# Fourier mixing and a gated feed-forward layer: moved set-up products, a turned row of weights by DMA, and another order at the start of batch 1

## The chip, the cores and the metric

The kernel runs on one core of a Trainium2 chip. A core has five engines with instruction streams of their own: TensorE (PE in the profile, with its weight loads shown apart as PEld), VectorE (DVE), ScalarE (ACT), GpSimd (POOL) and SyncE (SP), which here only issues transfers. Engines meet through semaphores. Matmuls write to eight banks of accumulator memory (PSUM); DVE and ACT read the banks and write to on-chip memory. Sixteen DMA engines move data between that memory and DRAM.

The metric is the device time of one execution in microseconds. Before the change the median of three runs is 631.07 us (631.01 to 631.09).

## The reference

`x` has 8 batches of 3008 rows and 256 channels. The real part of its two-dimensional Fourier transform goes through a gated layer:

```python
X = np.fft.fft(x, axis=1)
X = np.fft.fft(X, axis=2)
y = X.real.astype(np.float32).reshape(8 * 3008, 256)
gate = np.maximum(y @ w_gate, 0.0)      # w_gate: 256 x 1536
val = y @ w_val                         # w_val:  256 x 1536
return (gate * val @ w_out).astype(np.float32)   # w_out: 1536 x 256
```

## The kernel before

**Folding.** The transform over channels is multiplied into the weights once, in the set-up: `WA[i]` holds the cosine part and `WB[i]` the sine part of the gate weights (`i` = 0) and the value weights (`i` = 1), each 128 x 1536 in bf16. The transform over rows is a set of matmuls with tables of cosines and sines (`tabC`, `tabS`) on folded input. It gives for each batch `U` (cosine part) and `V` (sine part), 128 channels by 1505 columns. A column stands for two output rows, with a plus and a minus sign of the sine part. Channel 128, which the folding leaves alone, is a row of its own: `CB` holds it for all partitions, and `b2` holds its gate weights, which are row 0 of `WB[0]`, turned so that weight `f * 128 + p` stands in partition `p`, column `f`.

**Tiles.** The 1536 hidden channels are 12 tiles of 128 (`fi` = 0 to 11; `NF` = 12). Batch 0 goes through four segments of 376 or 377 columns (`blk` = 0 to 3), batches 1 to 7 through thirds of 512, 512 and 481 columns. For each tile, PE makes a gate product and a value product (`two`, L872: a `WA` and a `WB` matmul into one bank), and a `mirror` product (L877) that turns the plus sign into the minus sign in the same bank. ACT takes the ReLU of the gate (`relu`, L888), and DVE multiplies it with the value (`mult`, L897, or `relu_mult`, L908); the second of the two multiplies reads the value bank after its mirror product and frees it (`second`, `finish`).

**Banks.** `psO` has two banks (tag `o`), `psP` two (`p`), `psV` two (`v`), `psG` and `psD` one each (`g`, `d`). In the first segment the value product uses `d` for every third tile (`fi` 2, 5, 8, 11) and `v` for the others.

**Order.** The program's order is written by hand: each engine runs its own instructions in the order in which the code emits them. `todo_out` is a list of the products with `w_out` (L781, 256 columns each, into `o`) for finished blocks; `run(todo_out, n)` emits `n` of them. Before batch 1 (`paired` is False), `run` also calls `flush`, which emits the pending evictions: `fin` (L787) copies a full bank `o` to `os` on ACT (L794) and issues the stores to the output on SP (L806). From batch 1 on, evictions come one in each tile (`run_one(evict)`).

**Extra steps of batch 0.** The dictionary `more` (L825) gives steps by (segment, tile). `weights(1)` and `weights(2)` are four steps each for the second and the last third of the weights: two matmuls of 512 columns into a bank `o` (L427), and an eviction to `WA[i]` or `WB[i]` on ACT (L433, L429) or DVE (L431). The first third is made in `dft_first`. They stand at tiles 0 to 7 of segment 0. The last third of the weights is first used at tile 8. `even_table` steps follow from tile 8 on. `gate_128` (L833) stands at (2, 2): twelve matmuls with one column, row 0 of `WB[0]` as the stationary operand and a single 1.0 as the moving one, into bank `d`, and a DVE copy to `b2`.

**The transfers of SP** run in program order. The tile layer gives them eight semaphores in turn, so that a transfer also waits for the one eight before it. Around the change SP issues the loads for batch 1, two transfers of 768 KB that reverse the rows of batch 2 (`reverse`, L180), and then the stores of batch 0's first segment.

**From batch 1 on** a tile is a `slot` (L1029). The gate product of the next tile is made apart: `sine_part` (L1012) in the bank `g`, copied to on-chip memory by ACT (L1018); `cosine_part` (L1020) onto a bank `p` that ACT has seeded with channel 128 times `b2` (`seed`, L1005, L1010); `both` (L1024) makes the sum on DVE (L1026) and the difference on POOL (L1027). `slot` gets the current tile, the next (`mid`), the one after (`nxt`), whose gate it makes, and the one after that (`after`), which it seeds. The first gates of batch 1 (`ahead[0]` and `ahead[1]`) are made in the last tile of batch 0's last segment: `single_tile` (L940) calls the steps in `extra`, then the mirror product and ReLU of its gate, then `run(todo_out, outs)`, then the steps in `last` (L1141). `lead` marks the first tile of batch 1.

Of the kernel before, what the change touches and what calls it, by code (L numbers as in the profile page):

```python
# [11 lines left out]
F32 = mybir.dt.float32  # L12
BF16 = mybir.dt.bfloat16
I32 = mybir.dt.int32
F16 = mybir.dt.float16
ALU = mybir.AluOpType
# [13 lines left out]
def dram(ap, offset, pattern):  # L30
    return bass.AP(ap.tensor, offset, [list(p) for p in pattern])
# [3 lines left out]
def kernel(  # L35
# [8 lines left out]
    nc = tc.nc  # L44
    B, S, D = x.shape
    DF = moe_w_gate.shape[1]
    NF = DF // 128
# [12 lines left out]
    psD = ctx.enter_context(tc.tile_pool(name="psD", bufs=1, space=PS))  # L60
    ctx.enter_context(tc.manual_schedule())

    def single(name, shape, dt=F32, pool=const):
        return pool.tile(shape, dt, name=name, tag=name)
# [4 lines left out]
    WB = [single(f"WB{i}", [128, DF], BF16) for i in range(2)]  # L69
# [350 lines left out]
    def weights(c):  # L420

        f = slice(c * 512, (c + 1) * 512)

        def one(i, T, W):
            p = psO.tile([128, 512], F32, name="o", tag="o")
            for kc in range(2):
                nc.tensor.matmul(p[:], lhsT=T[:, kc, :], rhs=wr[i][c][:, kc, :], start=(kc == 0), stop=(kc == 1))  # L427
            if (i, c, W) == (0, 1, WA):
                return lambda: nc.scalar.copy(W[i][:, f], p[:])  # L429
            if (i, W) in ((1, WA), (c - 1, WB)):  # L430
                nc.vector.tensor_scalar(W[i][:, f], p[:], scalar1=1.0, op0=ALU.mult, scalar2=None)  # L431
            else:
                nc.scalar.copy(W[i][:, f], p[:])  # L433
        return [lambda i=i, T=T, W=W: one(i, T, W) for i in range(2) for T, W in ((TA, WA), (TB, WB))]
# [22 lines left out]
    for t in range(3):  # L457
        n = ROWS[1][t]
        p = slice(0, n)
# [43 lines left out]
    start_pool.__exit__(None, None, None)  # L503
    ch128 = nc.dram_tensor("ch128", (B, 4 * NJ + 1), BF16, kind="Internal").ap()
    b2 = single("b2", [128, NF])
    one = single("one", [1, 1], BF16)
    nc.vector.memset(one[:], 1.0)


    def even_table(n, c):  # L510
# [50 lines left out]
    def flush():  # L561
        for todo in (evict, sums):
            while todo:
                todo.pop(0)()
# [257 lines left out]
    fold_even()  # L822
    turns_and_rows()

    more = {(0, i): [s] for i, s in enumerate(weights(1) + weights(2))}  # L825
    for n, c in enumerate(even_order):
        for k, step in enumerate(even_table(n, c)):
            more.setdefault(divmod(EVEN_AT[n] + k, NF), []).append(step)
# [1 line left out]
    for seg in (2, 3):  # L830
        more.setdefault((1, 8 + seg), []).append(lambda seg=seg: minus_v(nc.scalar, seg))

    def gate_128():  # L833
        p = psD.tile([128, 512], F32, name="d", tag="d")
        for f in range(NF):
            nc.tensor.matmul(p[:, f:f + 1], lhsT=WB[0][0:1, f * 128:(f + 1) * 128], rhs=one[:], start=True, stop=True)
        nc.vector.tensor_scalar(b2[:], p[:, 0:NF], scalar1=1.0, op0=ALU.mult, scalar2=None)
    more[(2, 2)] = [gate_128]
    more_1 = {}
    for at, step in zip((-5, -4, -3, -2, -1, 7, 7, 8, 14, 17), channel_loads() + channel_turn()):  # L840
        (more_1 if at >= 0 else more).setdefault(at if at >= 0 else (3, NF + at), []).append(step)
# [5 lines left out]
    todo_out, todo_dft, todo_fold = [], [], []  # L847
# [3 lines left out]
    def run(todo, n):  # L851
        for _ in range(min(n, len(todo))):
            todo.pop(0)()
        if not paired:
            flush()

    def run_one(todo):
        if todo:
            todo.pop(0)()

    def run_fold(us):

        nonlocal credit
        credit = credit + us if todo_fold else 0
        while todo_fold and credit >= todo_fold[0][0]:
            cost, step = todo_fold.pop(0)
            step()
            credit -= cost
        if us > 50:
            credit = 0  # L870
# [6 lines left out]
    def mirror(bank, st, i):  # L877

        W, v = (WB, st["vm"]) if st["b"] == 0 else (WM, st["vs"])
        nc.tensor.matmul(bank[:, 0:st["n"]], lhsT=W[i][:, st["f"]], rhs=v, start=False, stop=True, skip_group_check=True)  # L880

    def bank(tag):
        return {"g": psG, "p": psP, "v": psV, "d": psD}[tag].tile([128, 512], F32, name=tag, tag=tag)
# [4 lines left out]
    def relu(st):  # L888
        st["r"] = space()
        nc.scalar.activation(st["r"][:, 0:st["n"]], st["g"][:, 0:st["n"]], ACTF.Relu)  # L890

    def half_h(st, sign):

        n = st["n"]
        return st["h"][:, 2 * n - 1:n - 1:-1] if sign else st["h"][:, 0:n]

    def mult(st, sign, r=None):  # L897
        n = st["n"]
        nc.vector.tensor_tensor(half_h(st, sign), (r or st["r"])[:, 0:n], st["v"][:, 0:n], op=ALU.mult)  # L899
# [8 lines left out]
    def relu_mult(st, sign):  # L908
        n = st["n"]
        nc.vector.scalar_tensor_tensor(half_h(st, sign), in0=st["s"][1 + sign][:, 0:n], scalar=0.0, in1=st["v"][:, 0:n],  # L910
                                       op0=ALU.max, op1=ALU.mult)

    def second(st):
        (relu_mult if "s" in st else mult)(st, 1)
        if st["n"] == 481:
            keep_rest(st)

    def finish(st):
        mirror(st["v"], st, 1)
        second(st)  # L920

    def value(st):
        st["v"] = bank("v")
        two(st["v"], st, 1)

    def gate(st, tag="g"):
        st["g"] = bank(tag)
        two(st["g"], st, 0)
        relu(st)
# [10 lines left out]
    def single_tile(st, outs, extra=(), last=(), tag="p"):  # L940

        gate(st, tag)
        if pending is not None:
            finish(pending)
        value(st)
        mult(st, 0)
        run(todo_out, outs)
        for step in extra:
            step()
        mirror(st["g"], st, 0)  # L950
        relu(st)
        run(todo_out, outs)
        for step in last:
            step()
        return st

    def first_tile(st, extra, outs):
# [47 lines left out]
    def seed(st, p=None):  # L1005

        if st is None or st["kind"] == "o":
            return
        st["p"] = p or bank("p")
        nc.scalar.activation(st["p"][:, 0:st["n"]], st["c"], ACTF.Copy, scale=b2[:, st["fi"]:st["fi"] + 1])  # L1010

    def sine_part(st):  # L1012
        n = st["n"]
        st["g"] = bank("g")
        nc.tensor.matmul(st["g"][:, 0:n], lhsT=WM[0][:, st["f"]], rhs=st["vs"], start=True, stop=True)  # L1015
        q = space()
        st["s"] = q, space(), q
        nc.scalar.copy(q[:, 0:n], st["g"][:, 0:n])  # L1018

    def cosine_part(st):  # L1020
        n = st["n"]
        nc.tensor.matmul(st["p"][:, 0:n], lhsT=WA[0][:, st["f"]], rhs=st["us"], start=False, stop=True, skip_group_check=True)  # L1022

    def both(st):  # L1024
        n, (q, sp, sm) = st["n"], st["s"]
        nc.vector.scalar_tensor_tensor(sp[:, 0:n], in0=q[:, 0:n], scalar=-0.5, in1=st["p"][:, 0:n], op0=ALU.mult, op1=ALU.add)  # L1026
        nc.gpsimd.tensor_tensor(sm[:, 0:n], sp[:, 0:n], q[:, 0:n], op=ALU.add)  # L1027

    def slot(cur, mid, nxt, after, outs, fold_us):  # L1029

        stop = len(todo_out)

        def out(part):
            run(todo_out, len(todo_out) - stop + outs * part // 8)
        old = nxt is not None and nxt["kind"] == "o"
        new = nxt is not None and not old
        if old:
            gate(nxt)
        lead = cur["lead"]
        if lead:  # L1040
            out(5)
        if new and mid["kind"] != "o":
            sine_part(nxt)
        out(3 if not lead else 5)
        out(5)
        if new and mid["kind"] == "o":
            sine_part(nxt)
        if new:
            cosine_part(nxt)
        seed(after)  # L1050
        if pending is not None:
            mirror(pending["v"], pending, 1)
        if pending is not None:
            second(pending)
        value(cur)
        if cur["kind"] == "o":
            mult(cur, 0, cur["first"])
        else:
            relu_mult(cur, 0)
        if new:  # L1060
            both(nxt)
        if old:
            nxt["first"] = nxt["r"]
            mirror(nxt["g"], nxt, 0)
            relu(nxt)
        run_fold(fold_us)
        run_one(evict)
        run_one(sums)
        out(8)
        return cur  # L1070
# [4 lines left out]
    for b in range(B):  # L1075
# [4 lines left out]
        for blk, block in enumerate(blocks):  # L1080
# [44 lines left out]
            if (b, blk) == (0, 0):  # L1125
                for fi in range(NF):
                    st = tile_of(block, fi, (U, V, CB))
                    add_h(st, hs)
                    if fi == 8:
                        todo_out = out_steps(b, block, hs, True)  # L1130
# [3 lines left out]
            elif not paired:  # L1134
                for fi in range(NF):
                    st = tile_of(block, fi, (U, V, CB))
                    add_h(st, hs)
                    tag = {(3, 8): "g", (3, 9): "d", (3, 10): "g", (3, 11): "d"}.get((blk, fi), "p")
# [8 lines left out]
                    if (blk, fi) == (1, 8):  # L1147
                        run(todo_out, len(todo_out))
                        todo_out = out_steps(b, block, hs, True)
                    pending = single_tile(st, 3 if blk == 1 else per_tile // 2, more_b.get((blk, fi), ()), last, tag)  # L1150
                    run(todo_dft, DFT_0[blk - 1][fi])
            else:
                for fi in range(NF):
# [4 lines left out]
                    outs = per_tile  # L1158
                    if (b, blk) == (B - 1, 2) and fi > 8:
                        outs = (10, 11, 17)[fi - 9]  # L1160
# [12 lines left out]
            if (b, blk) == (B - 1, 2):  # L1173
                todo_out = rest
            elif b or blk > 1:
                todo_out = out_steps(b, block, hs)
# [36 lines left out]
```

## Time and profile before

| | us |
|---|---|
| median of 3 runs | 631.07 |
| the profiled execution | 630.98 |
| its span in the profile | 629.2 |
| PE busy in it | 620.5 (99%) |
| DVE busy | 551.5 (88%) |
| POOL busy | 502.7 (80%) |
| ACT busy | 445.5 (71%) |

The span runs from the first to the last instruction of the program that the profiler shows; 1.8 us of the execution lie around it. In rows of the timeline the columns are start and length in microseconds, engine, line, operation, what it writes and reads, shapes, and how many instructions were merged into the row; in brackets the idle time of the engine ahead of it and what ended it. Matmuls are pipelined: the length of a row reaches to the modelled end of the matmul, while the next one has begun long before. So two starts have to be compared to see what a matmul costs. Batch 0 lies between about 19 and 104 us, batch 1 begins at about 105 us.

### The profile page before, as it was taken

The numbers are of one execution on the slowest core, as the hardware profiler recorded it, in microseconds if no ns is written. First come the engines' busy times: TensorE is split into PE (matmuls) and PEld (weight loads), VectorE is DVE, ScalarE is ACT, GpSimd is POOL, SyncE is SP. The second block draws the span as 40 slices with busy tenths as digits, with TensorE's granted clock in tenths as the row PEclk, the third lists the DMA queues.
The fourth block names the chain that finished last, engine by engine and source line by source line (L and its number), as shares of the span: only waits on it lengthen the run. The fifth ranks groups of instructions, "written<-read, shape, count | busy, mean of one in ns | idle before, by whom it ended". The sixth has DMA issues, their size and how long they took to land.

```text
span 629.2 us, 12441 instructions
## 1 busy us (share of the span) xinstructions
PE 620.5 (99%) x4114; PEld 398.4 (63%) x4114; DVE 551.5 (88%) x981; ACT 445.5 (71%) x813; POOL 502.7 (80%) x478
## 2 busy tenths in 40 slices
PE   8999999999999999999999999999999999999997
PEld 2566666566666666666666666666666666666666
DVE  8886676999899899988999999899999989999991
ACT  7796667777777767777777777777777777777762
POOL 8887992898999988799979989699886566666660
PEclk9999999999999999999999999999999999999999
DMA  9953748734264327315362426211221111211113
GB/s 240 209 206 118 173 177 102 182 73 151 82 150 145 126 76 183 113 44 165 83 187 64 140 76 130 68 50 36 77 61 38 42 60 56 57 38 51 51 44 102
DMA packets 82911, 66.47 MB, mean 106 GB/s; under 512 B 38517, under 2 KB 65941, under 8 KB 82846
## 3 DMA queue, kind: packets, MB, share of 16 engines
q1 hardware_dynamic: 78260, 60.01, 34.3%
q0 software_dynamic: 3984, 4.92, 3.9%
q10 hardware_dynamic: 602, 0.75, 0.4%
q8 instruction: 32, 0.52, 0.4%
q14 instruction: 33, 0.27, 0.2%
HBM read 41.88 MB, written 34.16 MB: 121 GB/s over the span
## 4 chain that ended last, share of the span: by engine, by line
PE 91%; DVE 4%; issue 2%; POOL 1%; DMA 1%; ACT 1%; DVEq 0%; ACTq 0%; POOLq 0%
PE o L781 36%; PE v L880 10%; PE v L875 9%; PE v L874 9%; PE g L1015 8%; PE p L1022 8%; PE d L585 4%; DVE h L910 2%; PE p L880 1%; PE p L874 1%; PE p L875 1%; DMA XG<-in_x_dram,gidx 1%; DVE h L899 1%; DVE r L1026 1%; POOL XG L120 1%
## 5 line engine op out<-in xcount | busy, mean ns | idle before, releaser
L1027 POOL TENSOR_TENSOR r<-r 128x512 f32<-128x512 f32 (+1 forms) x251 | 313.2, 1254 | 100.5 <-DVE r L1026 98.1
L910 DVE SCALAR_TENSOR_TENSOR h<-r,v 128x512 bf16<-128x512 f32 (+1 forms) x502 | 317.1, 673 | 39.2 <-PE v L880 26.5
L781 PE MATMUL o<-wo,h 128*128 128x256 bf16 x2172 | 330.6, 272 | 0.0
L781 PEld LDWEIGHTS <-h 128*128 128x128 bf16 x2220 | 216.7, 98 | 112.0 <-issue 1.3
L1010 ACT ACTIVATE p<-CB,b 128x512 f32<-128x512 bf16 (+1 forms) x251 | 171.8, 684 | 73.4 <-DVE r L1026 72.1
L1018 ACT COPY r<-g 128x512 f32<-128x512 f32 (+1 forms) x251 | 145.1, 578 | 66.5 <-PE g L1015 57.4
L1026 DVE SCALAR_TENSOR_TENSOR r<-r,p 128x512 f32<-128x512 f32 (+1 forms) x251 | 167.9, 669 | 0.9 <-ACT r L1018 0.9
L875 PE MATMUL v<-V,WB 128*128 128x512 bf16 (+3 forms) x296 | 108.6, 367 | 0.0
L874 PE MATMUL v<-U,WA 128*128 128x512 bf16 (+3 forms) x296 | 108.6, 367 | 0.0
L880 PE MATMUL v<-V,WM 128*128 128x512 bf16 (+1 forms) x252 | 94.4, 375 | 0.8 <-DVE h L910 0.4
L1015 PE MATMUL g<-V,WM 128*128 128x512 bf16 (+1 forms) x251 | 94.1, 375 | 0.5 <-ACT r L1018 0.4
L1022 PE MATMUL p<-U,WA 128*128 128x512 bf16 (+1 forms) x251 | 94.1, 375 | 0.2 <-ACT p L1010 0.2
L899 DVE TENSOR_TENSOR h<-r,v 128x376 bf16<-128x376 f32 (+2 forms) x90 | 46.2, 546 | 17.6 <-PE v L880 10.1
L874 PEld LDWEIGHTS <-WA 128*128 128x128 bf16 x348 | 33.9, 97 | 39.5 <-issue 10.4
L875 PEld LDWEIGHTS <-WB 128*128 128x128 bf16 x348 | 34.0, 98 | 34.3 <-DVE WB L431 0.6
L794 ACT COPY os<-o 128x512 f32<-128x512 f32 x92 | 52.6, 571 | 3.5 <-issue 3.0
L198 POOL TENSOR_TENSOR XG<-XG,XD 128x510 f32<-128x510 f32 x42 | 53.0, 1270 | 0.8 <-DMA XG<-xr 0.8
L890 ACT ACTIVATE r<-p 128x376 f32<-128x376 f32 (+1 forms) x80 | 38.0, 486 | 17.8 <-PE p L880 9.0
L206 POOL TENSOR_TENSOR AA<-XG 128x510 f32<-128x510 f32 x42 | 45.5, 1093 | 0.0
L1015 PEld LDWEIGHTS <-WM 128*128 128x128 bf16 x251 | 24.6, 98 | 5.7 <-issue 0.3
L1022 PEld LDWEIGHTS <-WA 128*128 128x128 bf16 x251 | 24.5, 98 | 3.7 <-issue 0.8
L880 PEld LDWEIGHTS <-WM 128*128 128x128 bf16 x253 | 24.8, 98 | 3.1
(186 smaller groups left out, 412.3 us busy)
## 6 DMA issues: line engine op xcount, KB each, us to landing
out_dram<-os SPq DMA_DIRECT2D x124, 128.0 KB
xr<-in_x_dram SPq DMA_DIRECT2D x12, 768.0 KB
XG<-xr SPq DMA_DIRECT2D x12, 768.0 KB
XD<-in_x_dram SPq DMA_DIRECT2D x15, 512.0 KB
out_dram<-os SPq DMA_DIRECT2D x35, 112.0 KB
XD<-in_x_dram SPq DMA_DIRECT2D x8, 448.0 KB
CB<-ch SPq DMA_DIRECT2D x7, 376.2 KB
out_dram<-os SPq DMA_DIRECT2D x13, 96.0 KB
```

Source lines behind the costliest of these rows:

```text
L198: e.tensor_tensor(XG[p, r, t, ::-1, 1:D], XG[p, r, t, ::-1, 1:D], XD[p, r, t, :, D - 1:0:-1], op=ALU.add)
L781: nc.tensor.matmul(st["p"][0:m, q, :], lhsT=lhs(f), rhs=wo[:, f, :], start=(f == 0 and not (early and q)), stop=(f == NF - 1), skip_group_ ...
L874: nc.tensor.matmul(bank[:, 0:st["n"]], lhsT=WA[i][:, st["f"]], rhs=st["us"], start=True, stop=False)
L875: nc.tensor.matmul(bank[:, 0:st["n"]], lhsT=WB[i][:, st["f"]], rhs=st["vs"], start=False, stop=True)
L880: nc.tensor.matmul(bank[:, 0:st["n"]], lhsT=W[i][:, st["f"]], rhs=v, start=False, stop=True, skip_group_check=True)
L910: nc.vector.scalar_tensor_tensor(half_h(st, sign), in0=st["s"][1 + sign][:, 0:n], scalar=0.0, in1=st["v"][:, 0:n], op0=ALU.max, op1=ALU.mult)
L1010: nc.scalar.activation(st["p"][:, 0:st["n"]], st["c"], ACTF.Copy, scale=b2[:, st["fi"]:st["fi"] + 1])
L1015: nc.tensor.matmul(st["g"][:, 0:n], lhsT=WM[0][:, st["f"]], rhs=st["vs"], start=True, stop=True)
L1018: nc.scalar.copy(q[:, 0:n], st["g"][:, 0:n])
L1022: nc.tensor.matmul(st["p"][:, 0:n], lhsT=WA[0][:, st["f"]], rhs=st["us"], start=False, stop=True, skip_group_check=True)
L1026: nc.vector.scalar_tensor_tensor(sp[:, 0:n], in0=q[:, 0:n], scalar=-0.5, in1=st["p"][:, 0:n], op0=ALU.mult, op1=ALU.add)
L1027: nc.gpsimd.tensor_tensor(sm[:, 0:n], sp[:, 0:n], q[:, 0:n], op=ALU.add)
```

## The change

Three things are changed.

1. `weights(2)` goes from tiles 4 to 7 of segment 0 to tiles 3 to 6. Tile 3 has two steps then, the last of `weights(1)` and the first of `weights(2)`.
2. `gate_128` goes, with its operand `one` and the memset that fills it. Instead, row 0 of `WB[0]` is stored to DRAM (`wrow`, 1536 values of 2 bytes) by a transfer that SP issues at tile (1, 1); at (1, 4) a second transfer reads it back so that each partition gets its 12 values (`brow`, 128 x 12), and at (2, 2) ACT copies `brow` to `b2`.
3. In the last tile of batch 0 the evictions are emitted after the steps of `last` instead of before them. In the slot of batch 1's first tile, `cosine_part` and `seed` come after the mirror and value products of the tile and its first multiply, instead of before them. For all other tiles `slot` and `single_tile` emit what they did, in the same order.

```diff
-    one = single("one", [1, 1], BF16)
-    nc.vector.memset(one[:], 1.0)
+    wrow = nc.dram_tensor("wrow", (1, DF), BF16, kind="Internal").ap()
+    brow = single("brow", [128, NF], BF16)
...
-    more = {(0, i): [s] for i, s in enumerate(weights(1) + weights(2))}
+    more = {(0, i): [s] for i, s in enumerate(weights(1))}
+    for i, step in enumerate(weights(2)):
+        more.setdefault((0, 3 + i), []).append(step)
...
-    def gate_128():
-        p = psD.tile([128, 512], F32, name="d", tag="d")
-        for f in range(NF):
-            nc.tensor.matmul(p[:, f:f + 1], lhsT=WB[0][0:1, f * 128:(f + 1) * 128], rhs=one[:], start=True, stop=True)
-        nc.vector.tensor_scalar(b2[:], p[:, 0:NF], scalar1=1.0, op0=ALU.mult, scalar2=None)
-    more[(2, 2)] = [gate_128]
+    more[(1, 1)].append(lambda: nc.sync.dma_start(out=wrow, in_=WB[0][0:1, :]))
+    more[(1, 4)].append(lambda: nc.sync.dma_start(out=brow[:], in_=dram(wrow, 0, [[1, 128], [128, NF]]), allow_slow_non_contiguous=True))
+    more[(2, 2)] = [lambda: nc.scalar.copy(b2[:], brow[:])]
...
         mirror(st["g"], st, 0)
         relu(st)
-        run(todo_out, outs)
+        for _ in range(outs):
+            run_one(todo_out)
         for step in last:
             step()
+        run(todo_out, 0)
         return st
...
         lead = cur["lead"]
-        if lead:
-            out(5)
+        out(4 if lead else 0)
         if new and mid["kind"] != "o":
             sine_part(nxt)
-        out(3 if not lead else 5)
-        out(5)
+        out(4 if lead else 5)
         if new and mid["kind"] == "o":
             sine_part(nxt)
-        if new:
+        if new and not lead:
             cosine_part(nxt)
-        seed(after)
+        if not lead:
+            seed(after)
         if pending is not None:
             mirror(pending["v"], pending, 1)
         if pending is not None:
@@
             mult(cur, 0, cur["first"])
         else:
             relu_mult(cur, 0)
+        if lead:
+            out(5)
+            cosine_part(nxt)
+            seed(after)
         if new:
             both(nxt)
```

With six products of `todo_out` for each tile there, `out(4)` and `out(5)` both mean three of them, so that the first three stay ahead of the sine product and the rest at the end of the slot.

## The prediction

> **What bounds the kernel now.** I read the shares of the page first, then its chain of waits, then the list of who waited for whom on TensorE up to 150 us, then the timeline of each place in that list.
>
> ```profile
> span 629.2 us, 12441 instructions
> PE 91%; DVE 4%; issue 2%; POOL 1%; DMA 1%; ACT 1%; DVEq 0%; ACTq 0%; POOLq 0%
> ```
>
> TensorE (PE) carries 91% of the chain that ends last. A microsecond taken out of PE's stream is therefore a microsecond of the kernel, unless something with a clock of its own holds PE later. The waits of PE (total, times, longest) between 0 and 150 us that this change can touch are these:
>
> ```profile
> PE g L1015 <- ACT r L1018: 0.4, 1, 0.4
> PE p L1022 <- ACT p L1010: 0.2, 1, 0.2
> PE d L875 <- DVE WB L431: 0.2, 1, 0.2
> ```
>
> They look small because a matmul's row lasts until its modelled end. The start of the next one shows the loss. With no wait, matmuls of 376 columns start 0.16 us apart, of 512 columns 0.21 to 0.22, of 256 columns (the `o` products) 0.11. The timeline of PE, tile 8 of batch 0's first segment, then DVE there:
>
> ```profile
> 29.94 0.32 PE L880 MATMUL p<-CB,WB 128*128 128x376 bf16 x1
> 30.10 0.32 PE L874 MATMUL d<-U,WA 128*128 128x376 bf16 x1
> 30.63 0.33 PE L875 MATMUL d<-V,WB 128*128 128x376 bf16 x1 [0.20 <-DVE WB L431]
> 28.98 0.53 DVE L899 TENSOR_TENSOR h<-r,d 128x376 bf16<-128x376 f32 x1
> 29.89 0.68 DVE L431 TENSOR_SCALAR WB<-o 128x512 bf16<-128x512 f32 x1
> ```
>
> The product due at 30.10 + 0.16 = 30.26 starts at 30.63, just behind the last eviction of weights (29.89 + 0.68 = 30.57). Loss: 0.37 us. The second place is the turning of channel 128's weights:
>
> ```profile
> 63.98 0.38 PE L781 MATMUL o<-wo,h 128*128 128x256 bf16 x2
> 64.29 0.45 PE L836 MATMUL d<-one,WB 1*128 1x1 bf16 x12
> 64.67 0.33 PE L880 MATMUL p<-CB,WB 128*128 128x376 bf16 x1
> ```
>
> The two `o` products are through at 63.98 + 0.21 = 64.19, and the next full product starts at 64.67: 0.48 us. The third is the start of batch 1, PE and then ACT:
>
> ```profile
> 104.74 0.49 PE L781 MATMUL o<-wo,h 128*128 128x256 bf16 x3
> 105.66 0.38 PE L1015 MATMUL g<-V,WM 128*128 128x512 bf16 x1 [0.44 <-ACT r L1018]
> 106.25 0.38 PE L1022 MATMUL p<-U,WA 128*128 128x512 bf16 x1 [0.21 <-ACT p L1010]
> 106.47 0.32 PE L880 MATMUL v<-CB,WB 128*128 128x377 bf16 x1
> 107.87 0.38 PE L1015 MATMUL g<-V,WM 128*128 128x512 bf16 x1
> 104.53 0.59 ACT L794 COPY os<-o 128x512 f32<-128x512 f32 x1
> 105.00 0.62 ACT L1018 COPY r<-g 128x512 f32<-128x512 f32 x1
> 105.47 0.73 ACT L1010 ACTIVATE p<-CB,b 128x512 f32<-128x512 bf16 x1
> ```
>
> The `o` products end at 104.74 + 0.33 = 105.07. The sine product waits 0.60 us for the copy that frees the one bank `g`, the cosine product another 0.37 for the seed of its bank. The eviction L794 stands ahead of both on ACT.
>
> **The change part by part. Weights a tile sooner.** Nothing is added: products of the last third move from tiles 4 to 7 into tiles 3 to 6, so tile 3 now has two groups. All positions from here are followed by hand with the spacing of rows: ACT copy 0.49 us before its successor starts, ReLU 0.38 to 0.40, DVE eviction 0.60, DVE multiply 0.46. Tile 3's second pair runs from 23.86 to 24.28; its input had landed by about 21. ACT gets a second copy at 24.55, and tile 4's ReLU moves from 24.55 to about 25.04. PE asks for that ReLU only at 26.15 (tile 4's mirror product), so the delay is hidden, with 0.6 us to spare. The DVE evictions of WA and WB fall to about 27.35 and 28.87, and the last weights are ready near 29.55 instead of 30.57.
>
> What is late next is bank `d`, which tile 8's value product reuses. It is freed by the DVE multiply that reads `d` (28.98 above). That multiply now has both evictions ahead of it and ends near 30.0. PE, with tile 7's pair gone and tile 3's added, reaches that product at about 30.03 and may wait 0.1; its second half then starts at 30.26. Gain **0.37**; with `d` half a microsecond later than I have it, nothing. The next input, `wo`, issued at 15.1, takes 15.1 us to land, at 30.2; its first use moves from 30.80 to 30.43, still behind it.
>
> **Twelve one-column products out.** PE gets 0.48 us back, but the mirror product that follows waits for a ReLU like those of the neighbouring tiles (a loss of 0.04 to 0.09 there), so I take **0.43**, with 0.38 (64.29 to 64.67 alone) and 0.48 as ends. A 0.16 us DVE copy goes. A 128x12 ACT copy comes, which no row shows; the 128x2 ones of L451 take 0.19, so 0.2. It stands on ACT between two ReLUs. The one ahead is needed by the mirror product and is not delayed; the one behind waits for that product anyway (0.4 to 0.9 us idle before these ReLUs). Cost: 0. The one-element memset of 0.06 us on DVE at 17.0 goes as well; I count nothing for it.
>
> **Two transfers in.** SP is idle from 32.3 on, so the 3 KB store of the row is issued there, a few microseconds after its last writer, and lies behind the two 768 KB transfers issued at 30.77. The read back is 1536 separate elements of 2 bytes. SP reaches it only after the sixth store of batch 0's outputs; it also waits for the row and for the transfer eight before it, so about 45.9:
>
> ```profile
> 45.15 0.70 SPq L806 DMA_DIRECT2D out_dram<-os  x2
> 52.13 0.82 SPq L806 DMA_DIRECT2D out_dram<-os  x2
> 101.50 6.08 SPq L133 DMA_DIRECT2D CX<-in_x_dram  x4
> ```
>
> [...] SP's next job is at 52.13. Four output buffers and about 5 us of slack cover it: cost 0. What it feeds is read at 64.2 at the earliest. [...]
>
> **Batch 1's first tile.** No instruction is added. The eviction L794 goes behind the next copy and seed on ACT. In the same hand count, the copy for tile 1 is at 104.74 (as soon as its product, begun at 104.31, is out) and ends at 105.34, so tile 2's sine product starts at 105.38 instead of 105.66. Behind it stand now the products that need nothing from ACT: mirror 105.59, value 105.75 and 105.97. Tile 2's seed runs 105.21 to 105.94 meanwhile, and the cosine product follows at 106.18 without a wait. Then three `o` products to 106.71, three of the transform to 107.19, and the next sine product at 107.19 instead of 107.87: **0.68**. Next in line: its bank is free at 106.93 (copy of tile 2 behind the eviction), its seed ends near 107.5 against a need at 107.7, and the eviction, 1.3 us later, feeds a store that SP could issue only at 107.6. If ACT came 0.4 us later, 0.28 would remain.
>
> Sum: 0.37 + 0.43 + 0.68 = **1.48 us**. Between the three places I found only waits that follow PE itself; the loads with their own clock have slack (the row `CB` for batch 1, issued at 91.80, is first read at 100.06). The profiled execution took 630.98 (span 629.2 and 1.8 around it), 0.09 under the median of 631.07. So 631.07 - 1.48 = **629.6 us**.
>
> **Rivals.** (A) *The weights' wait only changes its name*: bank `d` in place of WB. For it: DVE is busy without a gap from 27.9 to 32, and both evictions go ahead of the freeing multiply. Against: my count has 0.1 us. It leaves 1.48 - 0.37 = 1.11: about 630.0.
> (B) *The start of batch 1 keeps half its wait*: ACT has five jobs from 104.74 to 107.5 and PE one `g` bank. Price: only 0.28 of 0.68 is gained, so 1.08 in all, and 630.0.
> [...]
> (D) *More than the sum*: waits at 37.82, 43.04 and 60.54 (0.1 to 0.4 us each, for ACT and DVE) shrink with the new phase: 629.2.
>
> **How the numbers follow.** What a measurement of this kernel tells from no change is put at 0.2%, 1.26 us: faster means under 629.81. My forecast has 0.55, with 629.3 to 629.9 as its own range; about five sixths of it lies under the bound. A has 0.14, B 0.16 (both mostly within the bound), C 0.05, D 0.10. Faster 0.57, same 0.37, slower 0.06. The range reaches over A, B and D, and over A and B together (1.48 - 0.37 - 0.40, 630.4): 629.1 to 630.6.
>
> **What would show it.** Right: tile 8's second value product 0.16 to 0.25 us behind its first, no row of twelve 1x1 products and about 1.45 us between mirror products there, the first sine and cosine products of batch 1 without a wait of over 0.1 us, and every later stage earlier by 1.5. Wrong: a PE wait on the reader of `d` near 30; an ACT wait on DMA near 64; a new PE wait in the first four tiles of batch 1; or an advance of 0.8 us at 70 us that is gone by 100, which would mean that a load or POOL, not PE, sets the pace there.

## The result and the profile after

Over 14 runs each, the kernel before takes 631.00 us (630.84 to 631.25) and the changed one 629.87 (629.54 to 630.15): 1.13 us less, a ratio of 0.9981 with a 95% interval from 0.9974 to 0.9988. The forecast was 629.6, a gain of 1.48. The changed kernel's profiled execution took 629.88, with a span of 628.1 against 629.2. Its page, the first line and the chain that ended last:

```profile
span 628.1 us, 12374 instructions
PE 93%; DVE 3%; issue 1%; ACT 1%; DMA 1%; DVEq 0%; ACTq 0%
```

PE carries the chain still more than before (91%). The list of who waited for whom on PE, cut to 0 to 150 us (total, times, longest), without its lines for the start and for loads:

```profile
PE v L879 <- DVE h L898: 0.5, 2, 0.3
PE p L879 <- ACT r L889: 0.2, 1, 0.2
PE v L879 <- DVE h L909: 0.2, 1, 0.2
```

The three waits that the change was aimed at (on `g`, on the seed of `p`, on `WB`) are gone from this list. By the starts of the matmuls 0.29 us are still lost on `g`, as the prediction had it (105.07 to 105.38 there); e8_fill below takes that up. The wait on DVE's multiply (0.2 us, once, before the change) now makes 0.5 us in two. First the three places, in the timeline of the changed kernel, PE's rows and then those of DVE and ACT:

```profile
30.09 0.32 PE L873 MATMUL d<-U,WA 128*128 128x376 bf16 x1
30.24 0.32 PE L874 MATMUL d<-V,WB 128*128 128x376 bf16 x1
...
62.33 0.32 PE L879 MATMUL p<-CB,WB 128*128 128x376 bf16 x1
63.81 0.32 PE L879 MATMUL p<-CB,WB 128*128 128x376 bf16 x1
...
104.26 0.49 PE L781 MATMUL o<-wo,h 128*128 128x256 bf16 x3
104.88 0.38 PE L1016 MATMUL g<-V,WM 128*128 128x512 bf16 x1
105.68 0.38 PE L1023 MATMUL p<-U,WA 128*128 128x512 bf16 x1
106.71 0.38 PE L1016 MATMUL g<-V,WM 128*128 128x512 bf16 x1
...
28.90 0.68 DVE L431 TENSOR_SCALAR WB<-o 128x512 bf16<-128x512 f32 x1
29.50 0.53 DVE L898 TENSOR_TENSOR h<-r,d 128x376 bf16<-128x376 f32 x1
...
63.66 0.19 ACT L837 CAST b<-brow 128x12 f32<-128x12 bf16 x1
...
104.24 0.58 ACT L1019 COPY r<-g 128x512 f32<-128x512 f32 x1
104.72 0.70 ACT L1011 ACTIVATE p<-CB,b 128x512 f32<-128x512 bf16 x1
105.35 0.59 ACT L794 COPY os<-o 128x512 f32<-128x512 f32 x1
```

Tile 8's two products start 0.15 us apart instead of 0.53. The mirror products on both sides of the twelve one-column products are 1.48 us apart, as tiles without them are (1.95 before). At the start of batch 1 the sine product comes 0.62 us behind the first `o` product instead of 0.92, and the next sine product 1.83 us after it instead of 2.21.

What each place gave is read best as an *advance*: the start of a matmul in the profile before, less the start of the same matmul in the profile after.

| at (time in before) | advance, us | what lies between |
|---|---|---|
| 29.5 | 0.04 | |
| 30.8 | 0.40 | the weights: 0.36 |
| 65.06 | 0.87 | the one-column products: 0.47 |
| 67.2 | 0.42 | lost: 0.45 |
| 108.4 | 1.16 | the start of batch 1, with 0.06 regained before it |
| 200 | 0.95 | lost near 172: 0.2 |
| 250 to 550 | 1.18 to 1.15 | won near 222: 0.23 |
| 600 | 1.37 | won near 566: 0.22 |
| 617 | 1.00 | lost near 616: 0.37 |

Five of these rows (67.2, and all from 200 on) are about things the prediction did not speak of. The loss at 67 is the largest, and the timeline of the changed kernel shows where it begins, on DVE (PE, DVE, ACT):

```profile
64.91 0.32 PE L874 MATMUL v<-V,WB 128*128 128x376 bf16 x1
65.82 0.32 PE L874 MATMUL p<-V,WB 128*128 128x376 bf16 x1
66.44 0.32 PE L879 MATMUL v<-CB,WB 128*128 128x376 bf16 x1 [0.29 <-DVE h L898]
63.54 1.00 DVE L898 TENSOR_TENSOR h<-r,v 128x376 bf16<-128x376 f32 x2 [0.48 <-PE v L879]
65.38 1.00 DVE L898 TENSOR_TENSOR h<-r,v 128x376 bf16<-128x376 f32 x2 [0.84 <-PE v L874]
64.17 1.02 ACT L889 ACTIVATE r<-p 128x376 f32<-128x376 f32 x2 [0.32 <-PE p L879]
```

The multiply of 65.38 needs the first of the two ReLUs of 64.17, out at 64.66, and a value product of PE whose mirror partner is out by 64.91. Its wait, which the trace records as a semaphore instruction of its own, is met at 64.97. The multiply one tile earlier started 0.05 us behind its wait; this one starts 0.41 behind, 0.36 more. The bracket of its row names PE's product of 64.91, whose modelled end is 65.23; in e5_pad below the same multiply starts before that product's end, so it does not wait for it. From 64.97 on DVE waits for nothing that the profile shows. PE, which wants the result, starts its mirror product 0.62 us behind the last product (65.82 to 66.44) where 0.16 is the pitch.

### The profile page after: what moved, and what is told of

Same layout as the page of the kernel before. It is cut to its first block, busy times and chain, and to the rows that moved or that the text cites. A ratio compares the mean times of both kernels' runs of the same rounds, so it can differ in the third digit from the quotient of the medians.

```text
span 628.1 us, 12374 instructions
## 1 busy us (share of the span) xinstructions
PE 617.9 (98%) x4057; PEld 398.2 (63%) x4102; DVE 550.9 (88%) x979; ACT 445.8 (71%) x814; POOL 502.7 (80%) x478
## 4 chain that ended last, share of the span: by engine, by line
PE 93%; DVE 3%; issue 1%; ACT 1%; DMA 1%; DVEq 0%; ACTq 0%
PE o L781 37%; PE v L874 10%; PE v L879 10%; PE g L1016 8%; PE p L1023 8%; PE v L873 8%; PE d L585 4%; DVE h L909 2%; PE p L879 1%; PE p L873 1%; PE p L874 1%; PE v L395 1%; DMA XG<-in_x_dram 1%; DVE h L898 1%; DVE r L1027 1%
## 5 line engine op out<-in xcount | busy, mean ns | idle before, releaser
L873 PE MATMUL v<-U,WA 128*128 128x512 bf16 (+3 forms) x254 | 92.7, 365 | 0.0
L889 ACT ACTIVATE r<-p 128x376 f32<-128x376 f32 (+1 forms) x80 | 38.0, 486 | 17.8 <-PE p L879 9.6
```

What stands on the lines that cost most here:

```text
L873: nc.tensor.matmul(bank[:, 0:st["n"]], lhsT=WA[i][:, st["f"]], rhs=st["us"], start=True, stop=False)
```

## The experiments

In all of them a run of the kernel before stood on the same chip. "Late start" means: an instruction of DVE that begins about 0.40 us behind its wait although nothing that it reads is missing.

### e1_again: the changed kernel once more

No edit.

> The changed kernel once more, unedited, for a second profile. In the first one the advance over before is 0.39 us behind the weights, 0.85 behind the twelve products that went, but only 0.42 to 0.54 from 66.4 us on: DVE began one multiply at 65.38 although its waits had been met at 64.97, and PE waited 0.46 us for it at 66.44. Theory 'chance': such a late start (0.4 us) falls anywhere in an execution, and in another one it is elsewhere; then the advance between 67 and 100 us is 0.80 to 0.87 here. Rival 'place': it belongs to this spot of the changed program; then the advance is again 0.4 to 0.55 there. Time of both: 629.6 to 630.1, ratio 0.9975 to 0.9987.

629.93 us against 631.01, ratio 0.9982 [0.9973, 0.9991]. The advance goes -0.16, 0.19, 0.66 (65.06), 0.22 (67.2), 0.96 (108.4), 0.99 (250) to 0.85 (617). The first value is the start-up, which differs by 0.20 us between these two executions of one kernel (and by up to 0.6 us between the profiles of this document) and has nothing to do with the change; the steps after it are those of the first profile to within 0.04 us. The loss at 67 and the late multiply (65.58 here) belong to the kernel, not to one execution.

### e2_weights, e3_transfers, e4_start: each part alone, on the kernel before

```diff
e2:  -    more = {(0, i): [s] for i, s in enumerate(weights(1) + weights(2))}
     +    more = {(0, i): [s] for i, s in enumerate(weights(1))}
     +    for i, step in enumerate(weights(2)):
     +        more.setdefault((0, 3 + i), []).append(step)
e3:  the change's lines on one, wrow, brow, gate_128 and more[(1, 1)], more[(1, 4)], more[(2, 2)]
e4:  the change's lines in single_tile and slot
```

> Only the weights a tile sooner. Theory of the sum: 0.37 us faster, ratio 0.9994, with the value product of tile 8 at 30.24 and no loss behind it. Rival A (bank d takes the wait over): 0 to 0.15 us, and a PE wait for DVE near 30.

> Only the turning of channel 128's weights by transfers. Theory of the sum: 0.43 us faster, ratio 0.9993, and the advance of 0.4 to 0.46 holds from 65 us to the end. Rival 'place': the multiply behind it starts late again, 0.05 to 0.15 us faster, ratio 0.9998 or more. [...]

> Only the other order at the end of batch 0 and the start of batch 1. Theory of the sum: 0.68 us faster, ratio 0.9989 (in the first profile of the whole change the advance there grew by 0.62). Rival B: 0.28, ratio 0.9996.

| | median, us | before | ratio [95%] | advance |
|---|---|---|---|---|
| e2_weights | 630.64 | 631.01 | 0.9994 [0.9986, 1.0003] | 0.02, then 0.38 from tile 8 to the end (0.41) |
| e3_transfers | 630.82 | 631.01 | 0.9997 [0.9988, 1.0006] | -0.15, 0.32 at 65.06, -0.12 at 67.2, 0.06 at the end |
| e4_start | 630.20 | 631.01 | 0.9990 [0.9981, 0.9998] | 0.18, 0.86 at 108.4, 1.13 at the end |

Two of the three intervals reach 1, so the times alone do not show these parts; the steps of the advance do. The weights and the start of batch 1 are worth what they are worth in the whole change, 0.36 and 0.68 (the other 0.27 of e4_start's advance at the end come at 222, 320 and 566 us, taken together, and belong to what follows). The transfers win 0.47 and lose 0.44 again within 2.2 us, by themselves. So the loss at 67 is no collision of the three parts; it comes with the second. The timeline of e3_transfers, DVE and PE:

```profile
65.92 1.00 DVE L896 TENSOR_TENSOR h<-r,v 128x376 bf16<-128x376 f32 x2 [0.84 <-PE v L872]
66.98 0.32 PE L877 MATMUL v<-CB,WB 128*128 128x376 bf16 x1 [0.29 <-DVE h L896]
```

It is the same late multiply. To see what it has in common with others I numbered DVE's instructions, waits included, in the order of the traces. In the changed kernel late starts stand at numbers 191, 447, 703, 1343 and 1599 (65.38, 170.12, 269.97, 515.16, 614.17 us); before at 319, 575 and 1471 (119.30, 220.75, 564.98); in e2 at the same three numbers; in e3 at 191 and 959; in e4 at 831. DVE's rows in the kernel before:

```profile
119.30 0.69 DVE L910 SCALAR_TENSOR_TENSOR h<-r,v 128x512 bf16<-128x512 f32 x1 [0.30 <-PE v L875]
220.75 0.69 DVE L910 SCALAR_TENSOR_TENSOR h<-r,v 128x512 bf16<-128x512 f32 x1 [0.93 <-PE v L875]
564.98 0.69 DVE L910 SCALAR_TENSOR_TENSOR h<-r,v 128x512 bf16<-128x512 f32 x1 [0.42 <-PE v L875]
```

Every one is 63 plus a multiple of 128, right behind a wait. The changed kernel's trace has 13 such places. At the eight others nothing is seen: three are waits themselves (575, 959, 1471), and at five DVE goes on without idle time (63, 319, 831, 1087, 1215). Not every late start costs PE time: those at 119.30 before and at 269.97 and 515.16 after leave the advance as it is.

ACT has them too, which speaks against a cause in DVE's data. Its copy of `g` starts 0.04 us behind its wait as a rule. In the changed kernel one starts 0.32 behind (its wait met at 148.44, its start at 148.76), and that is ACT's instruction 319, again 63 plus a multiple of 128; in the kernel before it is 319 as well (149.60 to 149.92), in e3_transfers 575 and 831, in e4_start 1087 and 1215. The bracket of its row names POOL, but the distance is 0.32 at every one of these places. The timeline of the changed kernel, ACT:

```profile
148.76 0.58 ACT L1019 COPY r<-g 128x512 f32<-128x512 f32 x1 [1.07 <-POOL r L1028]
```

A second view points the same way, the list of DMA queues on the changed kernel's page (packets, MB, share of 16 engines):

```profile
q8 instruction: 32, 0.52, 0.4%
q14 instruction: 33, 0.27, 0.1%
```

33 loads of 0.27 MB are 8 KB each. They are not DVE's alone: the trace holds 4190 instructions of DVE, ACT, POOL and SP together, and 33 times 128 is 4224. The trace's DMA records give their times: one begins at 66.06, 170.90, 270.81 and 614.82, each 0.65 to 0.85 us *after* one of the late starts, and one at 516.51, 1.35 us after the fifth. This tie is loose: behind the late start at 119.30 of the kernel before, the next load begins only 3.2 us later. The theory from here on is an estimate from these counts, 63 plus multiples of 128 and 33 loads of 8 KB; no trace shows it as such: DVE's code comes in blocks of 128 instructions, the first instruction of a block starts 0.40 us behind its wait instead of 0.05, and this shows only where that instruction has just been waited for. The change took one memset and one copy out of DVE's stream and added one wait, so every instruction behind 64 us moved by one in the count.

### e5_pad: the changed kernel with the dropped memset kept

```diff
+    one = single("one", [1, 1], BF16)
+    nc.vector.memset(one[:], 1.0)
```

Nothing reads `one`. The rival was that ACT's new copy, or the order around it, holds the multiply.

> The changed kernel with one more DVE instruction in the set-up (the one-element memset at 17 us stays; nothing reads it). Theory 'code block': the late multiply is the DVE instruction that begins a block of 128 in DVE's stream (191st in the profiles of the changed kernel, of its repeat and of the transfers alone, each time right after a wait); one instruction more puts the wait itself there. Then no DVE row starts 0.4 us after its met wait at 65 us, the advance over before is 0.80 to 0.87 from 65 to 100 us and 1.4 to 1.5 behind the start of batch 1, and the late starts at 170, 270, 515 and 614 us go, while those of before at 220 and 565 us come back. Time 1.45 us under before, ratio 0.9977. Rival 'the ACT copy': the copy to b2 on ACT delays the multiply, wherever the instruction stands; then nothing changes: ratio 0.9982, late start at 65.4.

629.50 us against 631.06, ratio 0.9975 [0.9965, 0.9984]. The timeline of e5_pad, DVE and PE:

```profile
63.57 1.00 DVE L900 TENSOR_TENSOR h<-r,v 128x376 bf16<-128x376 f32 x2 [0.48 <-PE v L881]
65.05 1.00 DVE L900 TENSOR_TENSOR h<-r,v 128x376 bf16<-128x376 f32 x2 [0.48 <-PE v L881]
66.10 0.32 PE L881 MATMUL v<-CB,WB 128*128 128x376 bf16 x1
```

Number 191 is now the wait itself, and the multiply behind it starts 0.05 us after it. The late starts at 170, 270, 515 and 614 us are gone, and the three of the kernel before (319, 575, 1471) are back, as expected. PE's mirror product comes 0.25 us behind its predecessor, without a wait in brackets. The advance is 0.01, 0.36, 0.83, 0.75 (67.2), 1.44 (108.4) and 1.44 at the end. One instruction *more* on DVE, with the copy on ACT left in place, makes the kernel faster: the rival falls.

### e6_transfers_pad: the second part alone, with the memset kept

The edit is e3's without the removal of `one`.

> Only the transfers, with that memset kept. Code block: 0.40 to 0.45 us faster than before instead of 0.19, ratio 0.9993, advance 0.4 held from 65 to 100 us; a late start is possible at the 447th, 703rd, 831st, 1343rd or 1599th DVE instruction (about 170, 270, 320, 515 and 615 us). Rival ACT copy: 0.19 again.

630.68 us against 631.06, ratio 0.9995 [0.9986, 1.0003]. The advance is 0.30, 0.76, 0.68 (67.2) and 0.68 until 150: the loss of 0.36 is away. Then 0.48 (200), 0.72 (250 to 550), 0.94 and 0.57: with late starts at 447, 703, 1343 and 1599 it has the later losses of the changed kernel. Two late starts of e3_transfers (191 and 959) are gone and four others have come, so the time alone would not have shown the step.

### e7_slot_only: the third part without the eviction's move

The new order in `slot`, but `single_tile` as before, so that ACT's eviction stays ahead of the copy of `g`.

> Of the start of batch 1 only the slot's order, with the evictions of the last tile flushed where they were before. The eviction stays ahead of the copy that frees bank g, so the sine product waits as before (0.60 us), but the cosine product does not wait for its seed any more (0.37). Theory: 0.35 to 0.4 us faster, ratio 0.9994; the flush then accounts for the other 0.3. Rival: the eviction is not what holds ACT, and the whole 0.6 to 0.8 comes from the slot: ratio 0.9988.

630.48 us against 631.06, ratio 0.9990 [0.9982, 0.9999]. In its timeline PE still waits for the copy:

```profile
105.44 0.38 PE L1015 MATMUL g<-V,WM 128*128 128x512 bf16 x1 [0.43 <-ACT r L1018]
```

The advance grows by 0.37 there (0.23 to 0.60) instead of 0.68. So 0.37 of the third part is the place of the cosine product and of the seed, and the 0.31 left are the eviction, which was not moved alone.

### e8_fill: e5 with all six `o` products ahead of the first sine product

After the change, 0.29 us are still lost at 104.88 (three `o` products from 104.26 are through at 104.59). Three products more fill them:

```diff
-        out(4 if lead else 0)
+        out(8 if lead else 0)
```

> The changed kernel with the memset kept, and in the first slot of batch 1 all six output products ahead of the sine product instead of three. In the changed kernel that product still waits 0.30 us for the copy that frees bank g; the three products that fill the wait come from the end of the slot. Theory: 0.2 to 0.3 us under the changed kernel with the memset alone, ratio 0.9973 of before. Rival: the next sine product, then 0.32 us sooner, waits for its own bank instead: same time as with the memset alone.

629.11 us against 631.06, ratio 0.9971 [0.9960, 0.9982], the lowest median of all, though its interval and e5's overlap. The timeline of e8_fill, PE:

```profile
103.62 0.82 PE L783 MATMUL o<-wo,h 128*128 128x256 bf16 x6
104.27 0.38 PE L1018 MATMUL g<-V,WM 128*128 128x512 bf16 x1
105.08 0.38 PE L1025 MATMUL p<-U,WA 128*128 128x512 bf16 x1
105.83 0.38 PE L1018 MATMUL g<-V,WM 128*128 128x512 bf16 x1
```

The sine product follows six `o` products without a gap (103.62 to 104.27, 0.108 us each). The start gives 0.87 instead of 0.68, and the advance stays at 1.99 to 2.01 to the end. Of this 0.46 is the start-up of that execution (at 29.5), and the weights gave only 0.27 there: PE's first product with `wo` comes at 30.08, just behind the load of `wo`, which was issued at 15.3 and took 14.7 us to land. The 0.19 over e5 at the start of batch 1 is what this edit shows.

### e9_pad_late: the memset at 70 us instead of 17

```diff
+    one = single("one", [1, 1], BF16)
...
+    more.setdefault((2, 8), []).append(lambda: nc.vector.memset(one[:], 1.0))
```

> The changed kernel plus one memset of one element on DVE (a tile that nothing reads), as in e5, but placed near 70 us, after DVE's instruction 191, instead of at 17 us. Theory (what counts is how many instructions stand before a place in DVE's stream): the multiply near 65.4 us is still 0.40 us late (instruction 191 is not moved) and PE still loses 0.36 us more than before at 66.4; everything behind the memset moves by one, so the late starts near 170, 270, 515 and 614 us go and those near 220 and 564 of the kernel before return. Advance over the kernel before about 1.1 us from 108 us to the end; median 629.8 to 629.9, so 0.3 to 0.4 above e5. Rival (the memset at 17 us itself, or the layout of the start, is what helped e5): the late starts stay where the changed kernel has them, near 170, 270, 515 and 614 us; or the one near 65.4 goes too.

629.87 us against 630.89, ratio 0.9982 [0.9973, 0.9991]. The timeline of e9_pad_late shows late starts in four places (DVE, then PE):

```profile
65.50 1.00 DVE L900 TENSOR_TENSOR h<-r,v 128x376 bf16<-128x376 f32 x2 [0.84 <-PE v L876]
118.25 0.69 DVE L911 SCALAR_TENSOR_TENSOR h<-r,v 128x512 bf16<-128x512 f32 x1 [0.30 <-PE v L876]
219.70 0.69 DVE L911 SCALAR_TENSOR_TENSOR h<-r,v 128x512 bf16<-128x512 f32 x1 [0.92 <-PE v L876]
563.93 0.69 DVE L911 SCALAR_TENSOR_TENSOR h<-r,v 128x512 bf16<-128x512 f32 x1 [0.42 <-PE v L876]
66.56 0.32 PE L881 MATMUL v<-CB,WB 128*128 128x376 bf16 x1 [0.29 <-DVE h L900]
```

Ahead of the memset the changed kernel's late start is kept, with its loss (0.75 to 0.30); behind it the four of the changed kernel are gone and the three of the kernel before are back. The advance is 1.05 from 107 us to the end. It is the count of instructions ahead of a place that decides, not what the memset does at the start.

### e10_before_pads: the kernel before with its memset issued four times

```diff
-    nc.vector.memset(one[:], 1.0)
+    nc.vector.memset(one[:], 1.0)
+    nc.vector.memset(one[:], 1.0)
+    nc.vector.memset(one[:], 1.0)
+    nc.vector.memset(one[:], 1.0)
```

> The kernel before, unchanged but for the one-element memset at 17 us, which is issued four times instead of once (three more instructions of 0.06 us each on DVE). Theory: DVE's instruction 191 is now the multiply that started at 63.93 us in the kernel before, right behind its wait; it starts 0.40 us late, DVE's copy of the bias, the ReLUs behind it and the next pair of multiplies follow 0.40 us later, and PE's mirror product at 66.86 comes 0.3 to 0.4 us late. A late start of 0.40 us also appears at instruction 959, near 365 us, as in e3, and one near 614 us (1599). The late starts near 220 and 564 us stay. The kernel is 0.7 to 1.1 us slower than before: 631.7 to 632.1. Rival (three memsets cost their own time at most, at a place where DVE waits): no late start at 64 us, advance between -0.2 and 0.0 from 20 us to the end, median 631.0 to 631.2.

630.55 us against 630.89, ratio 0.9992 [0.9983, 1.0001]. I had expected a slower kernel, 631.7 to 632.1; it is not slower, and if anything faster. The timeline of e10_before_pads, DVE and PE:

```profile
64.46 1.00 DVE L903 TENSOR_TENSOR h<-r,v 128x376 bf16<-128x376 f32 x2 [0.84 <-ACT r L894]
369.56 0.69 DVE L914 SCALAR_TENSOR_TENSOR h<-r,v 128x512 bf16<-128x512 f32 x1 [0.42 <-POOL AA L206]
65.38 0.32 PE L879 MATMUL p<-V,WB 128*128 128x376 bf16 x1
65.54 0.32 PE L884 MATMUL v<-CB,WB 128*128 128x376 bf16 x1
```

The late starts at 191, 959 and 1599 (613.02) came where they were expected, 0.40 to 0.41 us behind their waits (64.05 for the first). PE lost nothing at any of them. At 64.46 a reason can be read, though no run tested it: the two multiplies are out at 65.46, and PE's mirror product that needs them comes at 65.54, and the twelve one-column products, still in this kernel, have held PE by 0.48 us. My price was wrong in a second point: I thought the late starts near 220 and 564 would stay, but three more instructions move those too. With them gone the advance goes from -0.16 to 0.07 at 222 and 0.28 at 566. Three memsets that do nothing for the result move the advance by 0.44, as much as one part of the change, through where the late starts fall; the time itself (0.34 us less) has an interval that reaches 1.

## Why the prediction was right, and where it was not

**Faster by a little: right, by less than the likeliest case had it.** 629.87 lies in the range (629.1 to 630.6) and 0.27 above the forecast. The gain is 1.13 us of 1.48. The prediction called faster what is under 629.81 and gave that 0.57; 629.87 is just on the other side, among the cases with 0.37. What the prediction left out cost 0.44 of the advance here and nothing in e5; which of the two comes hangs on one instruction, so it was chance that the loss stayed small enough for the range.

**Weights a tile sooner: 0.37 foreseen, 0.36 in the changed kernel, 0.36 in e2.** The DVE eviction is at 28.90 (28.87 worked out) and the reader of `d` ends at 30.03 (near 30.0). Rival A falls: PE goes from 29.90 to 30.09, so at most 0.03 us is lost on `d`.

**Twelve products out: 0.43 foreseen, 0.47 at 65.06.** It is 0.39 when the tiles behind it have settled (the 0.08 between 65.06 and 67.2 of e5), inside the ends of 0.38 and 0.48 that were given. ACT's copy cost 0, for the reason given: it sits between two ReLUs at 63.66.

**The transfers: cost 0, right.** SP issued the read at 46.01 (45.9 worked out) in 0.39 us, and the trace's DMA records show its 1536 pieces moved between 47.2 and 50.1 us. For the slack of about 5 us behind that cost, no run ahead of the result shows how long such an issue takes; the changed kernel showed 0.39 us, and 5.33 us from its end to SP's next store (46.40 to 51.73; that store was at 52.13 before). The copy that needs the read is at 63.66, with 13 us to spare: the late read to which the forecast gives 0.05 as C is shown by no run. What the prediction did not have is how late the row itself came: its store was issued from 32.35 on, its 3072 bytes moved only at 45.42, and the read waited for them (the list of who waited for whom on SP's queue, 25 to 60 us):

```profile
SPq L836 <- DMA wrow<-WB: 0.5, 1, 0.5
```

**Batch 1's start: 0.68 foreseen, 0.68 measured** in the changed kernel with e4 and e5. Rival B, half the wait kept, falls; e7 shows that it would have held without the eviction's move. That the eviction, 1.3 us later, costs nothing also held.

**The sum.** By e5, 0.36 + 0.39 + 0.68 = 1.43 us against 1.48, and e5's advance at the end is 1.44. The changed kernel's is 1.00. So the step that failed in a prediction that came right is the sentence behind the sum, "Between the three places I found only waits that follow PE itself", together with "I count nothing for it" for the memset. DVE's late starts of 0.40 us stand at 63 plus a multiple of 128 in its count, and which instruction that meets depends on how many stand ahead of it (191 is the multiply in the changed kernel and the wait ahead of it in e5). The change moved them by one: 0.36 lost at 66.4, then 0.2 lost near 172, 0.23 and 0.22 won near 222 and 566 (where the kernel before had late starts) and 0.37 lost at 616. Rival D, more than the sum, falls too: the advance stays at 0.40 from 35 to 60 us, so the waits that it named at 37.82, 43.04 and 60.54 did not shrink.

**What would show it.** The last sign named, an advance of 0.8 at 70 us gone by 100, came nearly as written (0.87 at 65.06, 0.42 at 67.2), but the cause I named for it, a load or POOL, was not it.

**What stays open.** Place and size are shown by the traces of all these kernels: 0.40 us behind a wait, at 63 plus a multiple of 128. That it is the change of code block is argued from the 8 KB loads, whose number fits blocks of 128 and which follow most of the late starts, not all, within 1.4 us; what DVE does in the 0.40 us no record shows. Something else that comes once in 128 instructions of an engine, the recording of the execution included, is not excluded. Nor was it tried which of the later losses PE would be spared by another count.

## What to carry to other kernels

Work out a change's gain place by place and compare starts in the two traces along the whole span; a place that gives what was worked out and a total that does not mean something else moved. When an engine begins 0.4 us behind a wait that the trace shows met, number its instructions before looking for a cause in the data: here one memset more ahead of it took the late start at 65.38 away (e5), three more took those at 220.75 and 564.98 away (e10), and such tests are cheap. Judge edits of under half a microsecond from the step in the advance and not from the total, which one memset shifted by 0.4 us here (629.87 with the changed kernel, 629.50 with e5).

## What the runs showed of the hardware

**Late starts at places 128 instructions apart.** On DVE a late start is 0.40 to 0.41 us behind a wait that is met; 5 of the 13 places at 63 plus a multiple of 128 show one in the changed kernel, 3 of 13 before. On ACT it is 0.32 us (148.44 to 148.76 in the changed kernel, at its instruction 319). The page of the changed kernel lists 33 loads of 8 KB in one queue of the kind `instruction` (`q14`) and 32 of 16 KB, 0.52 MB together, in the other (`q8`). That the late starts and the 8 KB loads belong together is the author's estimate from their number and times.

**The issue of the 3 KB row took 3.37 us.** The issue by SP, in the timeline of the changed kernel:

```profile
30.72 1.52 SPq L180 DMA_DIRECT2D xr<-in_x_dram  x2
32.35 3.37 SPq L835 DMA_DIRECT2D wrow<-WB  x1
46.01 0.39 SPq L836 DMA_DIRECT2D brow<-wrow  x1
```

It came behind two transfers of 768 KB; the read, of 1536 pieces, took 0.39 (0.70 in e3_transfers). The list of waits puts 3.1 us of it down to a ReLU of ACT (`SPq L835 <- ACT r L889`), from which the row takes nothing; what holds the issue no trace shows. SP's next transfer was at 41.35, behind ACT's copy to `os`, so it cost nothing here. At 68.99 in the kernel before, one output store behind the next pair of such transfers was issued in 8.03 us.
